# A folded DFT with its even rows split twice more, and one of its three products made once for seven sequences

## The chip, the cores and the metric

One core of a Trainium2 chip. The metric is the device time of one execution in microseconds (us). Before the change it is 2174.62 us, the median of three runs (2173.83 to 2174.92). The engines are named as in the profile: PE (matrix multiply), PEld (the weight loads of PE), DVE (vector), ACT (scalar), POOL (GpSimd), SP (the queue that issues most transfers).

## What is computed

Eight sequences of 3008 rows by 256 columns get a Fourier transform over the rows and one over the columns, of which the real part is kept. The result goes through two matrices with a squared ReLU in between.

```python
X = np.fft.fft(x, axis=1)            # x: (8, 3008, 256)
X = np.fft.fft(X, axis=2)
h = X.real.reshape(24064, 256) @ w_in        # (256, 2048)
g = np.maximum(h, 0.0) ** 2
out = g @ w_out                              # (2048, 256)
```

## The kernel before, in words

The transform over the 256 columns is folded into `w_in` at the start: `G1` and `G2` (128 and 127 rows by 2048) and a column `gE`. What is left of the transform is the DFT over the row index n, made separately for each sequence b.

**Symmetry.** The host lays the rows out so that row n comes with its three mirror rows (S - n, S/2 - n, S/2 + n), 1024 numbers in all, for n = 0 to 752. `fold` (six pieces `f_s` to `f_q` for each row tile, all on DVE) adds and subtracts these mirrors and the two column halves. It leaves two operands for each row tile: `wP` with 128 columns and one more (column H), and `wQ` with 127; each has an index `kp` for even and odd output frequency k.

**Products.** `dft_ops(b)` makes six groups: for kp = 0 and 1, three products named by `which`: 0 gives P (from `wP` and the cosine table), 1 gives Q (`wQ`, sine table), 2 gives E. E is one column, column H of `wP`, broadcast to 128 columns of weights so that its result stands on all 128 partitions. The rows lie as all even n (377) and then all odd n (376), three tiles of up to 128 rows each. In a group, `even_n` multiplies the three even tiles into a PSUM tile `pd` of 377 or 376 columns and ACT copies it to `da`; `odd_n` multiplies the three odd tiles, and DVE writes the sum of the two halves (L267) and, mirrored, their difference (L270, L272) into `Pt`, `Qt` or `Et`, tiles of 1505 columns in pairs of buffers (pool `pq`).

**Main loop.** There are 384 steps: 8 sequences by 6 blocks of 250 or 251 frequencies by 8 values of j. A step has `front` (two halves; each half multiplies G1 by Pt and G2 by Qt into PSUM tile `ph`, L292 and L293, and DVE forms `he` = Et * gE + P, then the two `g`, L295 to L298), `combine` (ACT: ReLU and square; POOL: four sums), and, two steps later, `back` (seven products with `w_out`, L332). After the last j of a block, `gather` combines the accumulators, and `store` transposes on PE (`po`, L366), copies on ACT (`os`, L368), and sends four transfers on SP (L370).

**What sets the order.** Each engine runs its instructions in the order of the program. The fold and the products of sequence b + 1 are a list of side pieces, each with a weight (0.7 for `f_s`, 1.2 for `odd_n`, and so on). `between`, called after each half of `front`, pops pieces at an even pace, so that the list is empty six halves before the sequence ends. Steps 0 to 7 of sequence 0 have no side pieces: there DVE prepares `w_out` (`load_wout`). The side work of sequence 0 itself (`ahead(0)`) runs before the main loop, with nothing beside it.

`pd` and `po` share two PSUM buffers (pool `psd`); `ph` has two of its own. Tiles of x stand in four buffers (`NX = 4`): `f_d` of tile t issues the load of tile t + 4 on SP (for sequence 0: on POOL's queue). SP issues in order too, and a transfer there waits until the one eight places ahead of it has landed.

Of the kernel before, what the change touches and what calls it, by code (L numbers as in the profile page):

```python
# [26 lines left out]

def row_tiles(S):  # L30

    q = S // 4
    tiles, at = [], 0
    for count in (q // 2 + 1, q // 2):
        assert 2 * P < count <= 3 * P
        for r in range(0, count, P):
            tiles.append((at + r, min(P, count - r)))
        at += count
    return tiles


@with_exitstack
def kernel(
# [23 lines left out]
    NT = 6  # L67
    NX = 4
    NK = (S // 8 + 1, S // 8)
    TILES = row_tiles(S)  # L70
    assert D == 2 * P and S % 16 == 0 and len(TILES) == NT and NROW == S // 4 + 1

    ctx.enter_context(tc.manual_schedule())
    const = ctx.enter_context(tc.tile_pool(name="const", bufs=1))
# [8 lines left out]
    op = ctx.enter_context(tc.tile_pool(name="op", bufs=2))  # L83
    psh = ctx.enter_context(tc.tile_pool(name="psh", bufs=2, space=PSUM))
# [7 lines left out]
    xt = {}  # L92

    def load_x(b, t):
        r0, rows = TILES[t]
        xt[b, t] = xp.tile([P, 4, D], F32, name="xt", tag="x")
        (nc.sync if b else nc.gpsimd).dma_start(out=xt[b, t][0:rows], in_=x[b, r0:r0 + rows])
# [4 lines left out]
    cosT = const.tile([P, 2, NT, NK[0]], F32, name="cosT")  # L102
    sinT = const.tile([P, 2, NT, NK[0]], F32, name="sinT")
# [11 lines left out]
    for kp in range(2):  # L115
        for tab, src in ((cosT, cos_s), (sinT, sin_s)):
            nc.gpsimd.dma_start(out=tab[:, kp], in_=src[:, kp])

    make_identity(nc, ident)

# [66 lines left out]

    folded = {}
    PQE = {}

    def fold(b, t):


        rows = TILES[t][1]
        r = slice(0, rows)
        st = {}

        def new(pool, nm, shape):
            st[nm] = pool.tile(shape, F32, name=nm, tag=nm)
            return st[nm]  # L200

        def f_s():
            v = xt[b, t]
            tt(out=new(fp, "fs", [P, 2, D])[r], in0=v[r, 0::2], in1=v[r, 1::2], op=ALU.add)

        def f_d():
            v = xt[b, t]
            tt(out=new(fp, "fd", [P, 2, D])[r], in0=v[r, 0::2], in1=v[r, 1::2], op=ALU.subtract)
            if b * NT + t + NX < B * NT:
                load_x(*divmod(b * NT + t + NX, NT))  # L210

        def f_sc():
            s, sc = st["fs"], new(fp, "sc", [P, 2, H + 1])
            nc.vector.tensor_copy(sc[r, :, 0:H + 1:H], s[r, :, 0:H + 1:H])
            tt(out=sc[r, :, 1:H], in0=s[r, :, 1:H], in1=s[r, :, D - 1:H:-1], op=ALU.add)

        def f_dc():
            d = st["fd"]
            tt(out=new(fp, "dc", [P, 2, H - 1])[r], in0=d[r, :, 1:H], in1=d[r, :, D - 1:H:-1], op=ALU.subtract)

        def f_p():
            sc, wP = st["sc"], new(wp, "wP", [P, 2, H + 1])
            for kp in range(2):
                tt(out=wP[r, kp], in0=sc[r, 0], in1=sc[r, 1], op=ALU.subtract if kp else ALU.add)

        def f_q():
            dc, wQ = st["dc"], new(wp, "wQ", [P, 2, H - 1])
            for kp in range(2):
                tt(out=wQ[r, kp], in0=dc[r, 0], in1=dc[r, 1], op=ALU.add if kp else ALU.subtract)
            folded[b, t] = (st["wP"], wQ)  # L230

        return [(0.7, f_s), (0.7, f_d), (0.5, f_sc), (0.4, f_dc), (0.6, f_p), (0.6, f_q)]

    def dft_ops(b):

        ops = []
# [5 lines left out]
        def group(kp, which, st):  # L242
            nk = NK[kp]
            n = P - 1 if which == 1 else P
            tab = sinT if which == 1 else cosT

            def product(half):
                ps = psd.tile([P, 512], F32, name="pd", tag="d")[0:n, 0:nk]
                for i in range(3):
                    t = 3 * half + i  # L250
                    rows = TILES[t][1]
                    w = folded[b, t][which % 2][0:rows, kp]
                    w = w[:, H:H + 1].to_broadcast([rows, n]) if which == 2 else w[:, 0:n]
                    nc.tensor.matmul(ps, w, tab[0:rows, kp, t, 0:nk],  # L254
                                     start=i == 0, stop=i == 2)
                return ps

            def even_n():
                ps = product(0)
                st["a"] = hp.tile([P, NK[0]], F32, name="da", tag="da", bufs=2)[0:n, 0:nk]  # L260
                nc.scalar.copy(st["a"], ps)

            def odd_n():
                ps = product(1)
                a, dst = st["a"], PQE[b][which]
                nh = S // 8
                tt(out=dst[:, kp:kp + 2 * nk - 1:2], in0=a, in1=ps, op=ALU.add)  # L267
                hi = dst[:, M - kp - 2 * (nh - 1):M - kp + 1:2][:, ::-1]
                if which == 1:
                    tt(out=hi, in0=ps[:, 0:nh], in1=a[:, 0:nh], op=ALU.subtract)  # L270
                else:
                    tt(out=hi, in0=a[:, 0:nh], in1=ps[:, 0:nh], op=ALU.subtract)  # L272
# [6 lines left out]
        return [(0.0, start)] + ops  # L279


    def front(b, k0, n, j, between):
# [194 lines left out]
```

## Time and profile before

| | before |
|---|---|
| median of three runs | 2174.62 us |
| the profiled execution | 2173.86 us, span 2172.1 us |
| PE busy | 2072.0 us, 95% of the span, 9504 matmuls |
| PEld busy | 1771.0 us, 82% |
| DVE busy | 1318.1 us, 61% |
| POOL busy | 1192.6 us, 55% |
| ACT busy | 927.5 us, 43% |

The sum of an engine's busy time over the span hides the stages: until about 115 us the kernel prepares `w_in`, folds sequence 0 and makes its products; until about 188 us it runs the first eight steps while DVE prepares `w_out`; from there on it is the main loop. Each product in fp32 shows in the profile as two matmul instructions and two weight loads, so 9504 matmuls are 4752 products. Matmuls overlap in the profile (a mean of 375 ns stands beside 212 ns from one start to the next), so PE's time is read from starts.

### The profile page before, as it was taken

The page shows a single profiled execution, that of the slowest core. Times are in us where ns is not written, and L with a number is a line of the kernel's source. Part 1 is how long each engine was busy: PE and PEld are TensorE (multiplying, and loading weights), DVE is VectorE, ACT ScalarE, POOL GpSimd, SP SyncE. Part 2 cuts the span into 40 slices and gives each one's busy share as a digit, 9 for nine tenths or more (in the row PEclk, how much of TensorE's full clock was granted, in tenths as well). Part 3 has the DMA queues.
Part 4 walks back from the last instruction along what each step waited for, and adds up shares of the span by engine and source line. Part 5 has one row for each costly group of instructions (what it writes and reads, how often), then busy time and mean ns, then how long its engine had stood idle before and what let it go on. Part 6 is the DMA issues. An engine that isn't in the chain of part 4 may idle for free.

```text
span 2172.1 us, 26892 instructions
## 1 busy us (share of the span) xinstructions
PE 2072.0 (95%) x9504; PEld 1771.0 (82%) x9504; DVE 1318.1 (61%) x3124; ACT 927.5 (43%) x1017; POOL 1192.6 (55%) x1776
## 2 busy tenths in 40 slices
PE   3668999999999999999999999999999999999998
PEld 1347888888888887888888888888888888888887
DVE  5588764677447764577546774477645775455553
ACT  0013443444445443444434444354434444344543
POOL 0046664566446654566545664466545665456655
PEclk8689999999999999999999999999999999999999
DMA  5211000111000100011001110011000000000000
GB/s 206 76 39 48 30 29 10 33 35 39 10 10 29 46 22 10 20 38 29 20 10 31 37 38 10 10 29 45 23 10 20 29 11 10 10 20 10 20 10 19
DMA packets 38371, 64.31 MB, mean 30 GB/s; under 512 B 3285, under 2 KB 27605, under 8 KB 37725
## 3 DMA queue, kind: packets, MB, share of 16 engines
q1 hardware_dynamic: 35981, 54.63, 8.3%
q0 software_dynamic: 1440, 7.72, 1.0%
q8 instruction: 74, 1.21, 0.2%
q14 instruction: 60, 0.49, 0.1%
q10 hardware_dynamic: 816, 0.26, 0.1%
HBM read 37.96 MB, written 24.64 MB: 29 GB/s over the span
## 4 chain that ended last, share of the span: by engine, by line
PE 93%; DVE 6%; issue 0%; ACT 0%; DMA 0%; POOL 0%; POOLq 0%; DVEq 0%
PE mC L332 15%; PE mA L332 15%; PE mB L332 15%; PE ph L293 15%; PE ph L292 15%; PE pd L254 8%; PE mD L332 7%; PE po L366 2%; PE pg L167 1%; DVE fs L153 1%; DVE fs L145 1%; DVE fs L139 1%; DVE fd L144 1%; DVE fs L151 0%; DVE fd L149 0%; DVE fd L143 0%
## 5 line engine op out<-in xcount | busy, mean ns | idle before, releaser
L295 DVE SCALAR_TENSOR_TENSOR he<-Et,gE,ph 128x251 f32<-128x251 f32 (+1 forms) x768 | 362.8, 472 | 673.9 <-PE ph L293 673.0
L306 ACT ACTIVATE g<-g 128x1004 f32<-128x1004 f32 (+1 forms) x384 | 399.4, 1040 | 825.1 <-DVE g L298 656.7
L312 POOL TENSOR_TENSOR s<-g 128x251 f32<-128x251 f32 (+1 forms) x384 | 243.4, 634 | 750.7 <-ACT g L307 671.0
L292 PE MATMUL ph<-Pt,G 128*128 128x251 f32 (+1 forms) x1536 | 455.6, 378 | 28.0 <-DVE g L298 27.9
L293 PE MATMUL ph<-Qt,G 127*128 127x251 f32 (+1 forms) x1536 | 455.4, 377 | 0.0
L307 ACT ACTIVATE g<-g 128x1004 f32<-128x1004 f32 (+1 forms) x384 | 399.2, 1040 | 12.2
L332 PE MATMUL mC<-s,wsum 128*128 128x251 f32 (+1 forms) x1536 | 390.3, 375 | 0.0
L332 PE MATMUL mA<-g,wout 128*128 128x251 f32 (+1 forms) x1536 | 389.9, 375 | 0.0
L297 DVE TENSOR_TENSOR g<-he,ph 128x251 f32<-128x251 f32 (+1 forms) x768 | 320.5, 417 | 58.8 <-DVE he L295 0.5
L292 PEld LDWEIGHTS ph<-Pt,G 128*128 128x128 f32 x1536 | 290.7, 190 | 77.8 <-DVE g L298 33.3
L293 PEld LDWEIGHTS ph<-Qt,G 127*128 127x128 f32 x1536 | 293.8, 191 | 36.9
L332 PEld LDWEIGHTS mA<-g,wout 128*128 128x128 f32 x1536 | 288.0, 190 | 42.2
L332 PEld LDWEIGHTS mC<-s,wsum 128*128 128x128 f32 x1536 | 291.9, 190 | 35.7
L298 DVE TENSOR_TENSOR g<-he,ph 128x251 f32<-128x251 f32 (+1 forms) x768 | 314.1, 409 | 0.0
L313 POOL TENSOR_TENSOR s<-s,g 128x251 f32<-128x251 f32 (+1 forms) x384 | 284.7, 741 | 30.1
L314 POOL TENSOR_TENSOR s<-g 128x251 f32<-128x251 f32 (+1 forms) x384 | 289.2, 753 | 0.0
L315 POOL TENSOR_TENSOR s<-g,s 128x251 f32<-128x251 f32 (+1 forms) x384 | 259.8, 676 | 0.0
L332 PE MATMUL mB<-g,wsum 128*128 128x251 f32 (+1 forms) x768 | 225.4, 374 | 0.0
L332 PE MATMUL mD<-s,wout 128*128 128x251 f32 (+1 forms) x768 | 225.0, 374 | 0.0
L332 PE MATMUL mB<-s,wout 128*128 128x251 f32 (+1 forms) x768 | 224.6, 374 | 0.0
L332 PEld LDWEIGHTS mB<-g,wsum 128*128 128x128 f32 x768 | 146.1, 190 | 17.9
L332 PEld LDWEIGHTS mD<-s,wout 128*128 128x128 f32 x768 | 144.9, 189 | 18.1
(63 smaller groups left out, 1351.5 us busy)
## 6 DMA issues: line engine op xcount, KB each, us to landing
xt<-in_x_dram SPq DMA_DIRECT2D x28, 512.0 KB
out_dram<-os SPq DMA_DIRECT2D x96, 125.0 KB
out_dram<-os SPq DMA_DIRECT2D x80, 126.0 KB
raw<-in_moe_w_in_dram SPq DMA_DIRECT2D x8, 512.0 KB
raw<-in_moe_w_out_dram SPq DMA_DIRECT2D x8, 512.0 KB
xt<-in_x_dram SPq DMA_DIRECT2D x7, 484.0 KB
xt<-in_x_dram SPq DMA_DIRECT2D x7, 480.0 KB
cosT<-in_cos_s_dram POOLq DMA_DIRECT2D x2, 1131.0 KB, 17.7
```

The lines of the kernel that those rows point to most:

```text
L292: nc.tensor.matmul(hP, G1[:, fs], pt[:, ks], start=True, stop=True)
L293: nc.tensor.matmul(hQ, G2[:, fs], qt[:, ks], start=True, stop=True)
L295: nc.vector.scalar_tensor_tensor(out=t, in0=et[:, ks], scalar=gE[:, fc:fc + 1], in1=hP, op0=ALU.mult, op1=ALU.add)
L297: tt(out=g[:, h, 0, 0:n], in0=t, in1=hQ, op=ALU.add)
L298: tt(out=g[:, h, 1, 0:n][:, ::-1], in0=t, in1=hQ, op=ALU.subtract)
L306: act(v, v, AF.Relu)
L307: act(v, v, AF.Square)
L312: gt(out=s1, in0=g21, in1=g22, op=ALU.add)
L313: gt(out=s2, in0=s1, in1=g11, op=ALU.subtract)
L314: gt(out=s3, in0=g11, in1=g21, op=ALU.subtract)
L315: gt(out=s4, in0=g12, in1=s2, op=ALU.subtract)
L332: nc.tensor.matmul(acc[nm][:, i, 0:n], w, v[:, 0:n], start=j == 0 and i == 0, stop=j == NJ - 1, skip_group_check=True)
```

## The change

**Rows in four classes.** `class_tiles` sorts the rows by n: n mod 8 = 0 (95 rows, one tile), n mod 8 = 4 (94 rows, one tile), n mod 4 = 2 (188 rows: tiles of 128 and 60), n odd (376 rows: 128, 128, 120). The layout in DRAM stays; the loads of x take every fourth or second row of the even part. So there are seven tiles of each sequence, not six, and `fold` runs once more for each sequence.

**Products in four pieces.** `even_n` makes three products into one PSUM tile `pd`: class 0 and class 1 with 95 (94) columns each, class 2 with 189 (188); ACT copies the first of them only. `join_4` (DVE) makes sum and mirrored difference of class 0 and 1 (to `db`), `join_2` those of `db` and class 2 (to `dc2`), and `odd_n` those of `dc2` and the odd rows, as before. `pd` is held from `even_n` to `join_2`.

**E in one pass.** For sequence 0, E is made as before. For sequences 1 to 7, `load_column` fetches column H of all seven sequences, number by number (28 transfers on SP, four in each of steps 8 to 14 of the program), `fold_column` folds it, and `dft_ops(None)` makes two groups with weights of seven columns. The result `e_rows` (7 x 1505) goes to DRAM (`e_dram`), and `load_e(b)` reads one row of it back to 128 partitions as `Et`. So a sequence has four groups, not six; sequence 1's list of side pieces has those two groups more, seven `fold_column` pieces and the write of `e_dram`.

**Buffers and tables.** x has three buffers (`NX = 3`). The tables are loaded class by class on POOL's queue in 24 transfers, not 4.

```diff
-    NX = 4
+    NX = 3
+    TILES = class_tiles(S)
+    NT = len(TILES)
...
-        r0, rows = TILES[t]
+        _, r0, step, rows = TILES[t]
         xt[b, t] = xp.tile([P, 4, D], F32, name="xt", tag="x")
-        (nc.sync if b else nc.gpsimd).dma_start(out=xt[b, t][0:rows], in_=x[b, r0:r0 + rows])
+        (nc.sync if b else nc.gpsimd).dma_start(out=xt[b, t][0:rows], in_=x[b, r0:r0 + step * (rows - 1) + 1:step])
...
+    def load_column(t):
+        _, r0, step, rows = TILES[t]
+        xe[t] = const.tile([P, 4, NE], F32, name=f"xe{t}")
+        for i in range(4):
+            nc.sync.dma_start(out=xe[t][0:rows, i], in_=x[1:B, r0:r0 + step * (rows - 1) + 1:step, i, H].rearrange("b r -> r b"))
+
+    def fold_column(t):
+        r = slice(0, TILES[t][3])
+        v = xe[t]
+        s = hp.tile([P, 2, NE], F32, name="es", tag="es", bufs=2)
+        tt(out=s[r], in0=v[r, 0::2], in1=v[r, 1::2], op=ALU.add)
+        we[t] = const.tile([P, 2, NE], F32, name=f"we{t}")
+        for kp in range(2):
+            tt(out=we[t][r, kp], in0=s[r, 0], in1=s[r, 1], op=ALU.subtract if kp else ALU.add)
...
             def even_n():
-                ps = product(0)
-                st["a"] = hp.tile([P, NK[0]], F32, name="da", tag="da", bufs=2)[0:n, 0:nk]
-                nc.scalar.copy(st["a"], ps)
+                st["ps"] = psd.tile([P, 512], F32, name="pd", tag="d")[0:n]
+                a = st["a"] = hp.tile([P, 2 * P], F32, name="da", tag="da", bufs=2)[0:n]
+                for c, at, nk in ((0, 0, n2), (1, n2, n2), (2, 2 * n2, n1)):
+                    product(st["ps"][:, at:at + nk], c)
+                nc.scalar.copy(a[:, 0:n2], st["ps"][:, 0:n2])
...
+            def join_4():
+                a, ps = st["a"], st["ps"]
+                st["b"] = hp.tile([P, 2 * P], F32, name="db", tag="db", bufs=2)[0:n, 0:n1]
+                both(st["b"][:, 0:n2], st["b"][:, n2:n1], a[:, 0:n2], ps[:, n2:2 * n2])
+
+            def join_2():
+                a, ps = st["b"], st["ps"]
+                st["c"] = hp.tile([P, NC[0][3]], F32, name="dc2", tag="dc2", bufs=2)[0:n, 0:n0]
+                both(st["c"][:, 0:n1], st["c"][:, n1:n0], a, ps[:, 2 * n2:2 * n2 + n1])
...
-            return [(0.6, even_n), (1.2, odd_n)]
+            return [(0.5, even_n), (0.5, join_4), (0.7, join_2), (1.2, odd_n)]
...
-            for which in range(3):
-                ops += group(kp, which, {})
+            for which in ((2,) if b is None else (0, 1) if b else (0, 1, 2)):
+                ops += group(kp, which)
+        if b is None:
+            ops.append((0.0, lambda: nc.sync.dma_start(out=e_dram[:, :], in_=e_rows)))
+        return ops
+
+    def load_e(b):
+        nc.sync.dma_start(out=PQE[b][2], in_=e_dram[b - 1:b].to_broadcast([P, NKT]))
...
     def ahead(b):
-        return [piece for t in range(NT) for piece in fold(b, t)] + dft_ops(b)
+        ops = [piece for t in range(NT) for piece in fold(b, t)] + dft_ops(b)
+        if b == 1:
+            ops += [(0.6, lambda t=t: fold_column(t)) for t in range(NT)] + dft_ops(None)
+        return ops + [(0.0, lambda: load_e(b))] if b else ops
...
+            if NJ <= i < NJ + NT:
+                load_column(i - NJ)
```

Three places show how instructions move. The first is PE at the end of the preparation, where the groups of sequence 0 are made (`pd`) and the main loop begins (`ph`). Before:

```order
L172 MATMUL pe<-altd,win 128x1 x8
L254 MATMUL pd<-cosT,wP 128x377 x6
L254 MATMUL pd<-sinT,wQ 127x377 x6
L254 MATMUL pd<-cosT,wP 128x377 x6
L254 MATMUL pd<-cosT,wP 128x376 x6
```

and now:

```order
L215 MATMUL pe<-altd,win 128x1 x8
L317 MATMUL pd<-cosT,wP 128x95 x2
L317 MATMUL pd<-cosT,wP 128x189 x2
L317 MATMUL pd<-cosT,wP 128x377 x3
L317 MATMUL pd<-sinT,wQ 127x95 x2
L317 MATMUL pd<-sinT,wQ 127x189 x2
L317 MATMUL pd<-sinT,wQ 127x377 x3
```

A group of six products of 377 columns has become seven: two of 95 columns, two of 189 and three of 377. All groups of all sequences have this form; those of E for sequences 1 to 7 have 7 output rows instead of 128.

The second is SP from the last loads of `w_out` (`raw`) to the first stores (`out_dram`), that is steps 8 to 14, where the tiles of sequence 1 are fetched (`xt`). Before:

```order
L128 DMA raw<-in_moe_w_out_dram 128x2x512 x8
L97 DMA xt<-in_x_dram 128x1024
L370 DMA out_dram<-os 126x256
L370 DMA out_dram<-os 125x256
L370 DMA out_dram<-os 126x256
L370 DMA out_dram<-os 124x256
L97 DMA xt<-in_x_dram 120x1024
```

and now (`xe` are the column's numbers, rows by sequences):

```order
L171 DMA raw<-in_moe_w_out_dram 128x2x512 x8
L243 DMA xe_954<-in_x_dram 95x7x1 x4
L133 DMA xt<-in_x_dram 60x1024
L243 DMA xe_994<-in_x_dram 94x7x1 x4
L243 DMA xe_1049<-in_x_dram 128x7x1 x4
L243 DMA xe_1092<-in_x_dram 60x7x1 x4
L133 DMA xt<-in_x_dram 128x1024
L455 DMA out_dram<-os 126x256
L455 DMA out_dram<-os 125x256
L455 DMA out_dram<-os 126x256
L455 DMA out_dram<-os 124x256
L243 DMA xe_1151<-in_x_dram 128x7x1 x4
```

The load of sequence 1's fifth tile (128 rows) and the stores of the first block now stand behind 16 transfers of single numbers; 12 more stand behind those stores.

The third is SP at the end of sequence 0, from the last stores of its fifth block on. Before:

```order
L370 DMA out_dram<-os 126x256
L370 DMA out_dram<-os 125x256
L97 DMA xt<-in_x_dram 128x1024
L370 DMA out_dram<-os 125x256 x2
L370 DMA out_dram<-os 124x256
L370 DMA out_dram<-os 125x256
```

and now:

```order
L455 DMA out_dram<-os 126x256
L455 DMA out_dram<-os 125x256
L360 DMA e_dram<-e_rows 7x1505
L364 DMA Et<-e_dram 128x1505
L133 DMA xt<-in_x_dram 60x1024
L455 DMA out_dram<-os 125x256 x2
```

The write of `e_dram` and the read of `Et` stand between the two stores; by the pace of the side pieces both are issued in step 45 of the 48, and `Et` is first read by DVE in the first step of sequence 1. For the later sequences the read alone stands there, issued in step 44.

More of the change, by code (lines that the diff above doesn't have):

```diff
@@ L39, in row_tiles, with class_tiles, column_counts, table_places @@
     return tiles
+def class_tiles(S):
+    half = S // 8 + 1
+    tiles = []
+    for c, order in enumerate((range(0, half, 4), range(2, half, 4), range(1, half, 2), range(half, S // 4 + 1))):
+        for r in range(0, len(order), P):
+            tiles.append((c, order[r], order.step, len(order[r:r + P])))
+    return tiles
+def column_counts(S):
+    counts = []
+    for kp in range(2):
+        n0 = len(range(kp, S // 4 + 1, 2))
+        n1 = (n0 + 1) // 2
+        n2 = (n1 + 1) // 2
+        counts.append((n2, n2, n1, n0))
+    return counts
+def table_places(S):
+    places, at = [], 0
+    for c, *_ in class_tiles(S):
+        places.append(at)
+        at += column_counts(S)[0][c]
+    return places, at
 @with_exitstack
@@ L83 @@
     op = ctx.enter_context(tc.tile_pool(name="op", bufs=2))
+    dp = ctx.enter_context(tc.tile_pool(name="dp", bufs=1, space=bass.MemoryType.DRAM))
     psh = ctx.enter_context(tc.tile_pool(name="psh", bufs=2, space=PSUM))
@@ L101 @@
     altd = const.tile([P, 2, 1], F32, name="altd")
-    cosT = const.tile([P, 2, NT, NK[0]], F32, name="cosT")
-    sinT = const.tile([P, 2, NT, NK[0]], F32, name="sinT")
+    cosT = const.tile([P, 2, WT], F32, name="cosT")
+    sinT = const.tile([P, 2, WT], F32, name="sinT")
     wout = const.tile([P, 2, NJ, D], F32, name="wout")
@@ L114 @@
         load_x(0, t)
-    for kp in range(2):
+    for t, (c, r0, step, rows) in enumerate(TILES):
         for tab, src in ((cosT, cos_s), (sinT, sin_s)):
-            nc.gpsimd.dma_start(out=tab[:, kp], in_=src[:, kp])
+            for i, (s0, count) in enumerate(row_tiles(S)):
+                mine = [r for r in range(count) if (s0 + r - r0) % step == 0 and 0 <= (s0 + r - r0) // step < rows]
+                if mine:
+                    o = (s0 + mine[0] - r0) // step
+                    nk = NC[0][c]
+                    nc.gpsimd.dma_start(out=tab[o:o + len(mine), :, PLACE[t]:PLACE[t] + nk],
+                                        in_=src[mine[0]:mine[-1] + 1:step, :, i, 0:nk])
     make_identity(nc, ident)
@@ L234, in dft_ops @@
     def dft_ops(b):
-        ops = []
         def start():
@@ L263, in odd_n @@
             def odd_n():
-                ps = product(1)
-                a, dst = st["a"], PQE[b][which]
+                ps = psd.tile([P, 512], F32, name="pd", tag="d")[0:n, 0:n0]
+                product(ps, 3)
+                dst = e_rows if b is None else PQE[b][which]
                 nh = S // 8
[L267 to L272, printed above, removed]
```

51 lines of the change are left out of this document (31 added, 20 removed).

## The prediction

> **What bounds the kernel now.** I read the page's part 1 first, then busy time by stretches of the span, then the list of waits, and only then single instructions in order of time. Part 1, and then four rows by stretches (from and to, length, then busy time with counts for PE, PEld, DVE, ACT, POOL, the granted clock, DMA share, GB/s):
>
> ```profile
> PE 2072.0 (95%) x9504; PEld 1771.0 (82%) x9504; DVE 1318.1 (61%) x3124; ACT 927.5 (43%) x1017; POOL 1192.6 (55%) x1776
> ```
>
> ```profile
> 77.40:95.00 17.60, 8.03 (x11) 2.80 (x12) 17.26 (x55) 0.47 (x1) 1.09 (x2) 0.60 0.50 156
> 95.00:116.00 21.00, 21.00 (x63) 12.40 (x62) 5.03 (x10) 2.36 (x5) 0.00 (x0) 0.93 0.19 66
> 195.00:275.00 80.00, 80.00 (x386) 71.21 (x385) 61.45 (x146) 39.70 (x43) 53.94 (x77) 1.00 0.13 40
> 1100.00:1400.00 300.00, 299.32 (x1382) 256.26 (x1381) 175.92 (x424) 134.70 (x149) 168.26 (x250) 1.00 0.08 23
> ```
>
> From about 195 us on PE is never idle and has its full clock, and DVE is busy 77% where sequence 1's side pieces run at their densest, 59% later. All PE waits of the loop are these two rows (total us, times, longest), and most of the first lies in the eight steps before 195 us:
>
> ```profile
> PE ph L292 <- DVE g L298: 27.9, 8, 5.7
> PE po L366 <- ACT os L368: 4.7, 7, 0.7
> ```
>
> So in the loop a microsecond of PE work taken away is a microsecond of span, until something else becomes late. Before the loop it is DVE's fold (77 to 95 us) and then PE's products (95 to 116 us) that set the pace.
>
> **What a product costs.** Matmul durations overlap, so I take starts. Six pd instructions, which are three products of 377 columns, and what follows; eight instructions of the transposes, which are four products of 128 columns; and, from the preparation, products of one column each with its own weight load:
>
> ```profile
> 38.45 1.84 PE L172 MATMUL pe<-altd,win 128*128 128x1 f32 x16
> ...
> 1041.09 1.04 PE L366 MATMUL po<-ident,c 128*126 128x128 f32 x8
> 1041.96 1.01 PE L332 MATMUL mA<-g,wout 128*128 128x251 f32 x4
> 1042.81 0.59 PE L332 MATMUL mB<-g,wsum 128*128 128x251 f32 x2
> ...
> 1051.31 2.07 PE L254 MATMUL pd<-cosT,wP 128*128 128x377 f32 x6
> 1053.22 1.01 PE L332 MATMUL mA<-g,wout 128*128 128x251 f32 x4
> ```
>
> 377 columns: 1.91 / 3 = 0.637 us. 251 columns: 0.85 / 2 = 0.425. Both are 1.69 ns a column. 128 columns: 0.87 / 4 = 0.218. One column: 1.84 / 8 = 0.23, so below some 128 columns the 128 columns of weights set the time, at 0.22. For 189 columns I take 0.320 (by columns), for 95 columns 0.22: by columns it would be 0.161, which is the lower bound, and the 0.425 of the 251-column product is an upper one for both. 0.22 has the nearest rows on both sides.
>
> **PE work in the loop.** The rows of the pd line give 576 instructions, so 288 products, 36 for each sequence:
>
> ```profile
> L254 PE MATMUL pd<-cosT,wP x384: 477/479/997, 79.9 to 1900.6; 128*128 128x377 f32 x64, 128*128 128x376 f32 x64, 121*128 121x377 f32 x16, 120*128 120x377 f32 x16
> L254 PE MATMUL pd<-sinT,wQ x192: 477/479/835, 95.7 to 1883.6; 128*127 128x377 f32 x64, 128*127 128x376 f32 x64, 121*127 121x377 f32 x16, 120*127 120x377 f32 x16
> ```
>
> A group costs 6 x 0.637 = 3.82 us before, and 2 x 0.22 + 2 x 0.320 + 3 x 0.637 = 2.99 now. The loop holds the groups of sequences 1 to 7: 42 before (160.5 us), 28 + 2 = 30 now (89.7 us; the two with seven weight columns stream as many columns). That is **-71 us**. With the lower bound for 95 columns it is -78, with the upper bound for both small products (group 3.61) -52.
>
> Had E stayed, 42 groups of 2.99 would have taken 35 us off; E's twelve groups fewer are the other half.
>
> **Before the loop: -1 us.** A tile's fold takes 2.9 us here, from one `fs` to the next, and there is a seventh:
>
> ```profile
> 77.45 0.69 DVE L204 TENSOR_TENSOR fs<-xt 128x512 f32<-128x512 f32 x1
> ...
> 80.35 0.68 DVE L204 TENSOR_TENSOR fs<-xt 128x512 f32<-128x512 f32 x1
> ...
> 94.31 1.63 PE L254 MATMUL pd<-cosT,wP 120*128 120x377 f32 x2 [1.26 <-DVE wP L224]
> ...
> 115.84 0.59 PE L292 MATMUL ph<-Pt,G 128*128 128x251 f32 x2
> ```
>
> The last product of the first group then starts 2.9 us later, at 97.2, and the five groups behind it take 5 x 0.83 = 4.2 us less: -1.3. Here the joins stand bare. A full-width join is 0.55 us on DVE, and the smallest operation of the fold 0.17:
>
> ```profile
> 78.67 0.17 DVE L214 COPY sc<-fs 128x4 f32<-128x4 f32 x1
> ...
> 96.05 0.55 DVE L267 TENSOR_TENSOR Pt<-da,pd 128x377 f32<-128x377 f32 x1 [1.18 <-PE pd L254]
> ```
>
> The four narrower joins lie between these two, so DVE needs 1.8 to 3.3 us for a group that takes PE 2.99. At the upper end PE waits for a PSUM buffer, 0.3 us in each of six groups, and some for the chain's latencies: bounds -3 and +4, taken -1. The 24 table loads on POOL's queue cost it 20 issues more at 0.53 us, 11 us, long before their first use at 79 us.
>
> ```profile
> 3.52 0.53 POOL L117 DMA_DIRECT2D cosT<-in_cos_s_dram  x1
> ...
> 79.05 0.55 POOL L97 DMA_DIRECT2D xt<-in_x_dram  x1 [72.83 <-DVE sc L214]
> ```
>
> ```profile
> xt<-in_x_dram POOLq DMA_DIRECT2D x1, 484.0 KB, 11.0
> xt<-in_x_dram POOLq DMA_DIRECT2D x1, 480.0 KB, 4.5
> ```
>
> With three x buffers the fourth tile is asked for at 79.05, lands 4.5 us later (alone on the queues; 11.0 was at the start, with everything in flight), and is wanted at 77.45 + 3 x 2.9 = 86.1. In the loop a load has more than 30 us. No cost.
>
> **DVE in sequence 0's loop: +2 us.** The loop's own work on DVE is these three in each half step (mean ns of one):
>
> ```profile
> L295 DVE SCALAR_TENSOR_TENSOR he<-Et,gE,ph 128x251 f32<-128x251 f32 (+1 forms) x768 | 362.8, 472 | 673.9 <-PE ph L293 673.0
> L297 DVE TENSOR_TENSOR g<-he,ph 128x251 f32<-128x251 f32 (+1 forms) x768 | 320.5, 417 | 58.8 <-DVE he L295 0.5
> L298 DVE TENSOR_TENSOR g<-he,ph 128x251 f32<-128x251 f32 (+1 forms) x768 | 314.1, 409 | 0.0
> ```
>
> The side list of sequence 1 weighs 46.1, where it weighed 31.8, over the same 40 steps: 1.45 times as dense. A step is 11 products of 0.425, so 4.68 us. In the 80 us from 195 the loop's own DVE work is 17.1 steps with two halves of 472 + 417 + 409 ns, 44 us, and 3 us of `gather`; 14 us are side pieces. At 1.45 times, DVE is busy 67 of 80 us, 84%. PE keeps two ph buffers ahead, so a burst is felt only where two pieces fall into one half. Bounds 0 and +10 (two waits of the 5.7 us above); taken +2. In the other six loops the side list weighs 36.1 over 48 steps, less dense than that of sequence 1 before (0.40 against 0.43 for each half), at which PE did not wait.
>
> **E through DRAM: +1 us.** Write and read are issued in step 45; until the first step of sequence 1 there are 2.5 to 3 steps, 12 to 14 us. `Et` is 753 KB: by the 480 KB row 7.1 us, by the 484 KB row 17 us; the write of 42 KB at most 4.5. Cover is just there; without it DVE's `he` waits, behind it every `g`, and PE after two ph products: at most some 8 us, once. Sequences 2 to 7 need only the read, with 15 us of cover. Likewise small: `pd` held while a `store` comes leaves one buffer for its two `po`; that happens in one place (step 27 of sequence 0), for one wait of the 0.7 us kind.
>
> **Column loads: 0.** 752 rows x 28 = 21,056 transfers of 4 bytes. The nearest row is the ACT queue in the first 5 us, where half-KB pieces and single numbers flow (packets, MB, share of 16 engines):
>
> ```profile
> q10 hardware_dynamic: 294, 0.14, 10.3%
> ```
>
> and the page's own rows for the whole span, where q1 is SP's queue:
>
> ```profile
> q1 hardware_dynamic: 35981, 54.63, 8.3%
> out_dram<-os SPq DMA_DIRECT2D x96, 125.0 KB
> out_dram<-os SPq DMA_DIRECT2D x80, 126.0 KB
> out_dram<-os SPq DMA_DIRECT2D x16, 124.0 KB
> xt<-in_x_dram SPq DMA_DIRECT2D x28, 512.0 KB
> xt<-in_x_dram SPq DMA_DIRECT2D x7, 484.0 KB
> xt<-in_x_dram SPq DMA_DIRECT2D x7, 480.0 KB
> raw<-in_moe_w_in_dram SPq DMA_DIRECT2D x8, 512.0 KB
> raw<-in_moe_w_out_dram SPq DMA_DIRECT2D x8, 512.0 KB
> ```
>
> 0.103 x 16 x 5 us / 294 = 28 ns a packet, the upper end; the lower is 0, and I take half, 14 ns, since 4 bytes are less than 512. Over all 16 engines the columns are 18 to 37 us, spread over seven steps (33 us). But they aren't spread evenly. Of q1's 35,981 packets, 24,064 are rows of out, 5271 rows of x and 4096 pieces of weights. 2550 are left over, and that is exactly what comes out if a transfer runs on as many engines as the largest divisor of its rows up to 16, with one closing packet on each: 125 rows on 5 (96 of these), 126 on 14, 124 on 4, 121 on 11, 120 on 15, 128 on 16. So the 95-row column goes over five engines and the 94-row one over two: 4 x (133 + 329 + 56 + 28 + 56 + 56 + 56) = 2856 numbers pass the busiest engine. The load of sequence 1's fifth tile stands behind 2184 of them. At 14 ns that is 31 us after step 8; the tile is wanted in step 19, 51 us after it. At 28 ns it is 61 us, and the sixth tile and the stores (two `os` buffers, ACT waiting in order) are late too: +16 us, the upper bound.
>
> The Trainium skill, "DMA: Bandwidth & Descriptors", section "Why a DMA increments its semaphore by 16 and not by 1", states this same divisor rule, and the 2550 packets agree with it. Its section "Rules for kernel authors" speaks against this change: a non-contiguous last dimension becomes one descriptor for each element and should be rearranged. No row here shows so many at once.
>
> **Sum.** -71 - 1 + 2 + 1 = -69, on the profiled execution's 2173.86: 2104.9. The median of the runs stands 0.76 above it: 2105.6, say **2106 us**, 3.2% faster.
>
> **Rivals.**
>
> *PE stays busy, but the joins leak (12%).* PSUM buffers are held over two to five halves, and each group's next product waits for `join_2`, DVE's joins for ACT's copy behind two activations. For it: three waits between engines where there was one. Against it: the copy's inputs come two halves earlier than its reader. Price: 30 groups x 0.7 us, the longest wait of this kind above, is 21 us: 2127.
>
> *Columns a little late (7%).* The 28 ns of the row: +16 us, 2122.
>
> *Columns dear (7%), slower than before.* For it: the two engines, and that transfers queue in order, so that x and the stores stand behind the columns. Against it: 28 ns is already a mean over larger packets. The columns end after 2856 numbers at a cost c each, 66 us (14 steps) may pass before the sixth tile is wanted, and the gain of 69 is gone where 2856 c - 66 = 69 us: from 47 ns on. At 60 ns the stall is 105 us: 2210.
>
> *Small products by columns (4%).* The 95-column products cost 0.161, PE saves 78 us, and the preparation -3: 2095. Against it: the 0.23 us of the one-column products.
>
> The forecast has the remaining 70%, from 2098 (the preparation at -3, DVE at 0, the 95-column products nearly half-way to 0.161) to 2114 (DVE at its upper bound).
>
> **Range and chances.** From 2098 to 2130: it holds the forecast, the leak, the mildly late columns and the upper bound of the small products (-52: 2125), and leaves out the dear columns and most of the last case. A difference of 0.2% (4 us) is what a measurement can tell. Faster 0.92, slower 0.07, and 0.01 between, where the columns cost just about 47 ns.
>
> **What the changed profile would show.** Right: three products of class 0 to 2 that start 0.22, 0.22, 0.32 us apart; 252 pd products in place of 288; PE busy at 99% or more in every stretch of the loop, DVE at 84% near 200 to 275 us; `ph` first at about 115 us. Wrong: DVE rows `fs` waiting for DMA `xt`, or ACT `os` waiting for its stores, between 240 and 330 us (the columns); DVE `he` waiting for DMA `Et` at a sequence's start (E); PE `pd` or `po` waiting for DVE joins or ACT in the loop (the leak). A loop in which PE is idle more than 2% would make the forecast wrong.

## The result: 2125.0 us, 2.3% faster, 19 us above the forecast

| | before | after |
|---|---|---|
| median | 2174.77 us (4 runs) | 2125.0 us (4 runs, 2123.76 to 2126.03) |
| ratio | | 0.9772, 95% interval 0.9755 to 0.9789 |
| span of the profiled execution | 2172.1 us | 2124.2 us |
| first `ph` | 115.84 us | 119.58 us |
| sequence 0 from step 8 to the first `ph` of sequence 1 | 215.7 us | 216.7 us |
| one of the sequences 1 to 6, from first `ph` to first `ph` | 253.5 us | 244.8 us |

The last three rows are differences of starts in the trace. They say where the 47.9 us of span went: 52.1 us were gained in the sequences 1 to 6 (8.7 in each) and 0.4 in the last one; 3.7 us were lost before the loop and 1.0 in sequence 0. Medians here and below are of the fast runs: one run of e_alone (3482 us) and one of efirst (4289 us) were far slower and do not count in them.

The profile of after, part 1, which answers to the first row of the prediction:

```profile
PE 2012.9 (95%) x9432; PEld 1740.2 (82%) x9432; DVE 1371.1 (65%) x3337; ACT 916.4 (43%) x1005; POOL 1223.2 (58%) x1797
```

72 matmul instructions fewer are 36 products fewer, 252 of `pd` where there were 288, as the prediction said. The table by stretches (from and to, length, then PE, PEld, DVE, ACT, POOL, granted clock, DMA share, GB/s), the stretches set at the same events as before: the fold, the products behind it, the dense side pieces, the middle of the loop:

```profile
78.40:98.20 19.80, 6.43 (x13) 2.85 (x13) 19.56 (x62) 0.24 (x1) 2.25 (x4) 0.59 0.37 117
98.20:119.60 21.40, 21.40 (x73) 13.05 (x74) 11.62 (x37) 1.19 (x5) 0.00 (x0) 0.82 0.30 85
195.00:275.00 80.00, 79.91 (x383) 70.55 (x383) 68.58 (x161) 37.83 (x41) 54.77 (x76) 1.00 0.28 47
1100.00:1400.00 300.00, 297.98 (x1420) 261.28 (x1419) 192.55 (x474) 137.89 (x151) 180.88 (x265) 1.00 0.09 29
```

DVE rose to 68.58 of 80 us, 86% (forecast 84%), and PE stayed busy beside it. In the middle of the loop PE was idle for 2.0 us of 300, where it had been 0.7. The second row shows the stage before the loop: its 21.4 us are what the same stage took before (94.3 to 115.8), at a lower mean clock (0.82, before 0.92).

The waits of PE (total us, times, longest):

```profile
PE ph L377 <- DVE g L383: 29.1, 8, 5.7
...
PE po L451 <- ACT os L453: 10.1, 15, 0.7
```

The first row is the one of before (27.9, 8, 5.7). The second was 4.7 us in 7 waits. No wait of PE for the new joins stands in the list inside the loop.

Two costs in the trace are larger than the forecast had them. The first is a group's first half. Here are the products of `even_n` for one group of sequence 2 in order of time (start, duration, engine, operation; x8 instructions are four products of 95, 94, 128 and 60 rows):

```profile
616.09 1.44 PE L317 MATMUL pd<-sinT,wQ 95*127 95x94 f32 x8
617.46 0.69 PE L377 MATMUL ph<-Pt,G 128*128 128x250 f32 x2
617.99 0.38 PE L378 MATMUL ph<-Qt,G 127*128 127x250 f32 x1
```

From the first start to that of `ph` it is 1.37 us, where 2 x 0.22 + 2 x 0.320 = 1.08 was forecast. The records of weight loads by shape (busy us, mean ns, then idle time before them and what ended it):

```profile
L317 PEld LDWEIGHTS pd<-sinT,wQ 60*127 60x127 f32 x32 | 4.9, 192 | 3.7 <-issue 3.7
```

The 60-row loads are as long as others, but the engine that loads stands idle before them, 3.7 us in 32, though nothing in the profile holds it. The single starts show what that costs. By columns, two instructions of 188 or 189 columns would start 0.16 us apart, as they do in cut65 below. Here the distance is 0.25 us from a 128-row one to a 60-row one, 0.26 between two 60-row ones, and 0.25 from a 60-row one to whatever follows: 0.28 us more. The product that follows is late once more: its two instructions start 0.32 us apart, and 0.21 elsewhere. Together that is 0.385 us for each group, so that a group costs 3.37 us.

The second is the store, where `pd` leaves one PSUM buffer for both `po`. PE in order of time, then ACT and DVE at the same place:

```profile
627.75 2.06 PE L317 MATMUL pd<-sinT,wQ 128*127 128x376 f32 x6
629.65 0.60 PE L451 MATMUL po<-ident,c 128*126 128x128 f32 x4
630.93 0.66 PE L451 MATMUL po<-ident,c 128*126 128x128 f32 x4 [0.68 <-ACT os L453]
631.42 1.01 PE L417 MATMUL mA<-g,wout 128*128 128x250 f32 x4
```

```profile
630.29 0.58 ACT L453 COPY os<-po 126x512 f32<-126x512 f32 x1 [2.85 <-PE po L451]
```

```profile
629.85 0.55 DVE L330 TENSOR_TENSOR Qt<-dc,pd 127x376 f32<-127x376 f32 x1 [0.28 <-PE pd L317]
630.32 0.54 DVE L332 TENSOR_TENSOR Qt<-pd,dc 127x376 f32<-127x376 f32 x1
```

`odd_n` was issued just ahead of `store`. Its `pd` holds one of the two `psd` buffers until DVE's second join ends at 630.86; the first `po` has the other until ACT's copy ends at 630.87. The second `po` starts at 630.93 and not at 629.65 + 2 x 0.22 = 630.09: 0.84 us lost.

Six of the fifteen waits are of this kind, with `odd_n` just ahead of the store, and so were all seven of before. In the other nine the `pd` of an `even_n` is still held for its joins, as the prediction said of step 27 of sequence 0. It happens in steps 27, 35 and 43 of sequence 0, and in step 35 of each of the sequences 1 to 6. At 338 us, PE, ACT and DVE:

```profile
338.00 0.66 PE L451 MATMUL po<-ident,c 128*126 128x128 f32 x4 [0.68 <-ACT os L453]
```

```profile
337.36 0.58 ACT L453 COPY os<-po 126x512 f32<-126x512 f32 x1 [2.74 <-PE po L451]
```

```profile
338.02 0.35 DVE L332 TENSOR_TENSOR dc<-pd,db 127x188 f32<-127x188 f32 x1
```

PE goes on 0.06 us behind ACT's copy, while DVE's `join_2` is still reading `pd`. Both kinds cost 0.84 us: fifteen are 12.6 us in the whole kernel; the seven of before were 5.9.

### The profile page after: what moved, and what is told of

The parts are those of the page before. It is cut to its first block, busy times and chain, and to the rows that moved or that the text cites. A ratio compares the mean times of both kernels' runs of the same rounds, so it can differ in the third digit from the quotient of the medians.

```text
span 2124.2 us, 26994 instructions
## 1 busy us (share of the span) xinstructions
PE 2012.9 (95%) x9432; PEld 1740.2 (82%) x9432; DVE 1371.1 (65%) x3337; ACT 916.4 (43%) x1005; POOL 1223.2 (58%) x1797
## 4 chain that ended last, share of the span: by engine, by line
PE 92%; DVE 7%; ACT 0%; issue 0%; DMA 0%; POOL 0%; POOLq 0%; ACTq 0%; DVEq 0%
PE ph L377 15%; PE mA L417 15%; PE mC L417 15%; PE mB L417 15%; PE ph L378 15%; PE mD L417 7%; PE pd L317 6%; PE po L451 2%; PE pg L210 1%; DVE fs L196 1%; DVE fs L188 1%; DVE fd L187 1%; DVE fs L182 1%; DVE fs L194 0%; ACT os L453 0%; DVE fd L192 0%
## 5 line engine op out<-in xcount | busy, mean ns | idle before, releaser
L397 POOL TENSOR_TENSOR s<-g 128x251 f32<-128x251 f32 (+1 forms) x384 | 252.0, 656 | 687.2 <-ACT g L392 653.1
L378 PE MATMUL ph<-Qt,G 127*128 127x251 f32 (+1 forms) x1536 | 455.6, 377 | 0.0
L378 PEld LDWEIGHTS ph<-Qt,G 127*128 127x128 f32 x1536 | 294.5, 192 | 36.6
L399 POOL TENSOR_TENSOR s<-g 128x251 f32<-128x251 f32 (+1 forms) x384 | 290.5, 757 | 0.0
```

The costliest lines, as they stand in the source:

```text
L378: nc.tensor.matmul(hQ, G2[:, fs], qt[:, ks], start=True, stop=True)
L397: gt(out=s1, in0=g21, in1=g22, op=ALU.add)
L399: gt(out=s3, in0=g11, in1=g21, op=ALU.subtract)
```

## The experiments

Each was timed in several rounds beside the kernel before on the same chip; its median was 2174.77 us beside after, 2174.79 beside the next four and 2174.83 beside the others. Medians with the ratio to it:

| kernel | median us | ratio, 95% interval | span us |
|---|---|---|---|
| after | 2125.0 | 0.9772 [0.9755, 0.9789] | 2124.2 |
| cut65 | 2115.7 | 0.9727 [0.9713, 0.9742] | 2113.8 |
| cut64 | 2125.0 | 0.9771 [0.9757, 0.9786] | 2122.9 |
| hold21 | 2111.4 | 0.9710 [0.9695, 0.9724] | 2109.9 |
| e_alone | 2125.2 | 0.9772 [0.9753, 0.9792] | 2122.8 |
| cut65_hold21 | 2100.1 | 0.9658 [0.9644, 0.9673] | 2097.9 |
| split_alone | 2169.6 | 0.9975 [0.9966, 0.9985] | 2166.1 |
| before_hold | 2167.7 | 0.9968 [0.9956, 0.9981] | 2165.3 |
| efirst | 2089.4 | 0.9606 [0.9590, 0.9622] | 2087.9 |

### Is it the rows of the small tile? cut65 and cut64

The 188 rows of class 2 are cut differently; the number of products, their columns and the data stay the same.

```diff
-        for r in range(0, len(order), P):
-            tiles.append((c, order[r], order.step, len(order[r:r + P])))
+        step = 123 if c == 2 else P
+        for r in range(0, len(order), step):
+            tiles.append((c, order[r], order.step, len(order[r:r + step])))
```

That is cut65: 123 and 65 rows in place of 128 and 60. In cut64 the number is 124, so 124 and 64 rows.

> The change with its 188 rows of class 2 cut into tiles of 123 and 65 rows, not 128 and 60; nothing else. Theory (rows): a tile of at most 64 rows makes PE load its weights without overlap. In the changed kernel's loop the 189-column instructions of such a group take 253, 264 and 250 ns to the next start where 189 columns at 0.845 ns are 160, together 0.29 us a group. Expected: all of these at 160 to 190 ns, 28 groups x 0.29 = 8 us less in the loop, 1.5 less before it: 2115 (2113 to 2117). Rival (short products): products of 189 columns cost 0.25 us for each instruction whatever their rows; then no difference from 2125.

> The same cut one row away: tiles of 124 and 64 rows. Theory (rows, with the limit at 64): as slow as the change, 2125 (2123 to 2127), with 250 to 264 ns again. Rival (few rows cost, without a limit): close to the kernel with 65 rows, within 2 us of it.

cut65 took 2115.7 us, 9.3 less than after; cut64 2125.0, no difference. A single row decides. The same group of sequence 2 in cut65, and its weight loads:

```profile
613.39 1.25 PE L318 MATMUL pd<-sinT,wQ 95*127 95x94 f32 x8
614.48 0.59 PE L378 MATMUL ph<-Pt,G 128*128 128x250 f32 x2
614.90 0.59 PE L379 MATMUL ph<-Qt,G 127*128 127x250 f32 x2
```

```profile
L318 PEld LDWEIGHTS pd<-sinT,wQ 65*127 65x127 f32 x32 | 5.9, 199 | 0.0
```

In cut64:

```profile
614.57 1.44 PE L318 MATMUL pd<-sinT,wQ 95*127 95x94 f32 x8
615.94 0.69 PE L378 MATMUL ph<-Pt,G 128*128 128x250 f32 x2
616.47 0.59 PE L379 MATMUL ph<-Qt,G 127*128 127x250 f32 x2
```

```profile
615.43 0.29 PEld L318 LDWEIGHTS pd<-sinT,wQ 64*127 64x127 f32 x2 [0.22 <-issue]
```

With 65 rows the four products take 1.09 us, the 1.08 of the forecast, and the loads follow each other without a gap (0.0 idle in 32). With 64 rows it is 1.37 us again, as with 60. So the forecast's prices for 95 and for 189 columns were right, and the cost lies in the number of rows. From the group's first start to that of the second product behind it (L379 here, L378 in after) it is 1.51 us, where after has 1.90: 0.39 us. The loop agrees: each of the sequences 1 to 6 has four such groups and takes 243.24 us, 1.54 less than in after, which is 4 x 0.385. Sequence 0 is 1.3 us shorter from step 8 on, so that the loop gained 10.6 us; the spans differ by 10.4, the medians by 9.3.

### Is it the store? hold21

`between` holds a piece back when a store is near: `even_n` two steps ahead or less, `odd_n` one step ahead or less.

```diff
+        due = (3 - i) % NJ
         while side and spent <= 0:
+            name = side[0][1].__name__
+            if name == "even_n" and due <= 2 or name == "odd_n" and due <= 1:
+                return
             t, f = side.pop(0)
```

> The change, but a group's even_n is not begun in the two steps before a store or in its step, and odd_n not in the step before or in its step, so that both transposes of a store find their own free PSUM buffer. Theory (leak at the stores): 15 waits of PE for the copy of os, 0.75 us each, go: PE po <- ACT os from 10.1 us on PE (and the weight loads' 13.7) to 0, the time 10 to 11 us lower, 2114 to 2115. Rival (the pieces held back only come bunched elsewhere and DVE makes PE wait there): within 3 us of 2125, with PE ph <- DVE g above 35 us.

2111.4 us, 13.6 less than after. That is more than the 10 to 11 expected, which went by 0.75 us a wait; by the starts, 15 x 0.84 are 12.6. PE's waits, cut to those for DVE's `g` and those of `po`, and then the store of the same block in order of time:

```profile
PE ph L377 <- DVE g L383: 29.1, 8, 5.7
...
PE po L451 <- POOL c L438: 2.5, 1, 2.5
```

```profile
621.79 1.04 PE L451 MATMUL po<-ident,c 128*126 128x128 f32 x8
```

No wait for ACT's copy is left (the wait for POOL is the last store of the kernel and stands in before too), and the eight instructions of the store run in one piece.

### The two halves of the change: e_alone and split_alone

e_alone is the kernel before with E in one pass: its six tiles and two classes, groups of 6 x 0.637 us, three x buffers, but columns, `fold_column`, `e_dram` and `load_e` of the change. Its result stands in the first rows of sequence 1's `Et`, not in a tile of its own, before it goes to DRAM. split_alone is the change without the pass: E is made for each sequence, with no columns and no transfers through DRAM.

```diff
 # e_alone, beside the new functions of the change
+    return [(0 if r0 <= S // 8 else 3, r0, 1, rows) for r0, rows in row_tiles(S)]
 # split_alone
-            for which in ((2,) if b is None else (0, 1) if b else (0, 1, 2)):
+            for which in range(3):
...
-            if NJ <= i < NJ + NT:
-                load_column(i - NJ)
```

> The kernel before, with E of seven sequences in one pass and through DRAM, but rows in two classes as before (six tiles, groups of six products of 377 columns) and three x buffers. Theory: twelve groups fewer of 3.82 us, 45.8 us, and nothing given back except up to 2 us in sequence 0's loop: 2129 to 2131. Rival (the columns or the trip through DRAM cost in the loop of sequence 0 or at its end): above 2135.

> The change without its E pass: rows in four classes, three groups of seven products for each kp of every sequence as E is made for each sequence. Theory: a group costs 3.28 us as measured in the change, not 3.82, 42 groups in the loop, 23 us less; against it 14 more waits at the stores of 0.84 us, 12 us, 3.7 us before the loop, and some 1 us in the loop of sequence 0: 2168 (2164 to 2172), so that nearly all of the change's gain is the E pass. Rival (the split carries half of the gain, as the forecast had it): 2140 or less.

E alone takes 2125.2 us, as much as the whole change and 4 us less than was expected of it; the split alone takes 2169.6, 5 us less than before. PE's waits at stores in e_alone, and in split_alone:

```profile
PE po L427 <- ACT os L429: 0.7, 1, 0.7
```

```profile
PE po L451 <- ACT os L453: 13.5, 20, 0.7
```

So E's pass gives more than its arithmetic: twelve groups of 3.82 us are 45.8, and six waits fewer than before (7 to 1) are 5.0, 50.8 in all for a measured 49.6. Which pieces fall beside a store changes with the list, and here it changed for the better. The split is the reverse. Its 42 groups save 35 us by the forecast; the small tile takes 42 x 0.385 = 16.2 back, thirteen waits more take 10.9, and its first `ph` comes at 118.27, 2.4 us late. That leaves 5.5 us, and 5.2 are measured.

### Both mends: cut65_hold21

> Both mends on the change: class 2 as tiles of 123 and 65 rows, and the pieces held back around a store. Theory (two separate costs on PE): they add up, 9.3 and 13.6 us as measured one by one, 2102 (2100 to 2104). Rival (the two overlap, or DVE or the start of the loop becomes the limit): 2106 or more.

2100.1 us, 24.9 below after, where 9.3 and 13.6 are 22.9. In the loop they add exactly: the sequences 1 to 6 are 3.33 us shorter than in after, and apart it was 1.54 and 1.79. But for the last store, the only waits of PE in its loop are the ones in the steps before 195 us:

```profile
PE ph L378 <- DVE g L384: 28.8, 8, 5.8
```

Each of the sequences 1 to 6 takes 241.45 us in it, 12.0 less than before. Two groups fewer (2 x 3.82) and four cheaper by 0.83 account for 11.0 of them, and the one wait of before for 0.84; 0.2 us are left over.

### Did the kernel before have the same leak? before_hold

The lines of hold21, put into the kernel before.

> The kernel before with nothing but even_n and odd_n held back around a store in the same way. Theory: its 7 waits at the stores cost 0.84 us each, 6 us less: 2169 (2167 to 2171). Rival (holding back itself speeds up or slows down something else): outside of that.

2167.7 us, 7.1 less than before (seven waits by 0.84 are 5.9). The wait of 4.7 us that the prediction quoted was a cost of before, not the background of the loop:

```profile
PE ph L292 <- DVE g L298: 27.8, 8, 5.7
...
PE po L366 <- POOL c L353: 2.5, 1, 2.5
```

### A version beyond both: efirst

The E pass is moved out of sequence 0's loop into the preparation: it is made for all eight sequences; the columns are loaded between pieces of `w_in`, folded in DVE's stretch of its third chunk, and multiplied where PE waits for DVE. Class 2 is cut 96 + 92, and the stores are held as above.

```diff
-    NE = B - 1
+    NE = B
...
+        for t in {1: (0, 1), 2: range(2, NT)}.get(c, ()):
+            load_column(t)
+        if c == 3:
+            for _, f in e_ops[:4]:
+                f()
...
+        if c == 2:
+            for t in range(NT):
+                fold_column(t)
...
-    for _, f in ahead(0):
+    first = ahead(0)
+    for _, f in first[:6] + e_ops[4:] + first[6:]:
```

> Class 2 as tiles of 96 and 92 rows, pieces held back as before, and E made for all eight sequences in one pass during the preparation: the column's numbers are loaded between the pieces of w_in, folded while DVE waits for PE there, and the two groups run while PE waits for DVE. Theory: against 2102 for both mends, the two E groups leave the loop (5.9 us) and two groups of sequence 0 leave the preparation (6.8 us), with up to 2.5 us of DVE joins added there: 2092 (2088 to 2096). Rival (the column loads delay w_in, on which DVE waits in the preparation): above 2098.

2089.4 us, 10.7 below cut65_hold21 and 3.9% below before. The stretch of the preparation that took up the work, in efirst and then in after:

```profile
40.00:80.00 40.00, 21.58 (x92) 12.23 (x91) 26.96 (x73) 3.38 (x7) 0.57 (x1) 0.74 0.40 51
```

```profile
40.00:80.00 40.00, 16.97 (x59) 9.75 (x59) 21.70 (x43) 2.50 (x5) 0.00 (x0) 0.66 0.05 14
```

PE and DVE were idle for 23 and 18 of these 40 us in after; in efirst they do 4.6 and 5.3 us more in the same time. The first `ph` comes at 113.72 us (117.53 in cut65_hold21), and sequence 0 from step 8 takes 205.1 us (212.0): the two E groups, at the 3.27 us each that they take in cut65, are 6.5 of these 6.9. The other sequences take the same 241.45 us in both.

## Why the prediction was right, and where it was not

**The form of the argument held.** A microsecond of PE work taken from the loop was a microsecond of span, and nothing else became the bound. 2125.0 is inside the range; it is 19 us above the forecast, and in the spans the loss is 21.1 us: -47.9 measured, -69 by the sum. (The profiled execution of after was 1.0 us above its median, that of before 0.9 below.)

**"What a product costs", the 0.320 for 189 columns: this step failed.** For 95 columns 0.22 held, for 377 columns 0.637 too (627.75 to 629.65 is 1.90 for three). The 189-column products were priced by columns alone; with 60 rows one of the two costs 0.385 us more, between itself and its neighbours. A group was 3.37 us and not 2.99. In "PE work in the loop" the -71 was therefore mis-sized: 30 x 0.385 = 11.5 us of it were not there. cut65 shows it. The prediction's upper bound for both small products, by which -71 becomes -52, contained this, but it was set by the 251-column row, and not by any thought of rows. That the loop's measured gain is 52.1 + 0.4 is chance: part of it is the next point.

**"That happens in one place", one more wait of `po`: this step failed.** The prediction looked at the list of sequence 0 and costed the wait by the page's 0.7 us. The place that it named is there, but a `pd` held for its joins meets a store in nine places, and one meeting of the kind that before had is gone: eight waits more than before, at 0.84 us each, are 6.7 us against the 0.7 in the +1. That `pd` is held through three pieces was seen; that two more stores of sequence 0 and one in each of the sequences 1 to 6 meet it was not. The rival "the joins leak" named the right pool and the wrong reader. It had each group's own next product wait for `join_2`, and no such wait shows inside the loop; `po` waits instead, for ACT's copy, which the prediction had named as a sign of the leak. Its time of 2127 is near the result by chance: the waits are 12.6 us in all, not 21 more, and the small tile is no part of it.

**"Before the loop: -1": wrong in sign.** The first `ph` came 3.7 us later. The rows of after: fold, last product of the first group, the last two groups and first `ph`:

```profile
78.45 0.69 DVE L266 TENSOR_TENSOR fs<-xt 95x512 f32<-95x512 f32 x1
```

```profile
98.15 1.63 PE L317 MATMUL pd<-cosT,wP 120*128 120x377 f32 x2 [1.26 <-DVE wP L286]
...
112.84 3.53 PE L317 MATMUL pd<-sinT,wQ 95*127 95x94 f32 x14
116.21 3.54 PE L317 MATMUL pd<-cosT,wP 95*128 95x94 f32 x14
119.58 0.59 PE L377 MATMUL ph<-Pt,G 128*128 128x251 f32 x2
```

The fold began 1.0 us later (78.45, before 77.45). That is not the change's doing: in cut65 it began at 78.95, in cut65_hold21 at 77.40. The seventh tile cost its 2.9 us (19.70 from fold to last product, 16.86 before). But the five groups behind it took 21.43 us, and before 21.53: the 4.2 us of the forecast did not come. The clock tells half of it. In after and then in before, two stretches around its rise:

```profile
104.00:106.00 2.00, 2.00 (x5) 1.08 (x4) 0.00 (x0) 0.00 (x0) 0.00 (x0) 0.56 0.18 58
106.00:108.00 2.00, 2.00 (x11) 1.35 (x10) 1.12 (x3) 0.24 (x1) 0.00 (x0) 1.00 0.13 50
```

```profile
96.00:98.00 2.00, 2.00 (x4) 1.08 (x4) 1.01 (x2) 0.00 (x0) 0.00 (x0) 0.52 0.99 357
98.00:100.00 2.00, 2.00 (x8) 1.14 (x7) 0.00 (x0) 0.47 (x1) 0.00 (x0) 1.00 0.47 180
```

PE has a granted clock of 0.50 until about 105.8 us in after, until about 97.9 in before. Behind the first group that is 7.6 us at half speed, where it was 3.6: 2.0 us more lost. At full clock a group takes 3.37 us here (from 112.84 to 116.21), 0.38 over the 2.99 of the forecast; for five that is an estimated 1.9, and the two make 3.9 of the 4.1 us that are missing. Only part of it is the small tile's: from fold to first `ph` it is 40.9 to 41.1 us in the four kernels that split the rows and have a tile of 60 or 64 (after, cut64, hold21, split_alone), and 40.1 and 40.4 in the two with 65. Why the clock rose later was not tested. It goes with the rows in four classes: in these six it rose between 104.2 and 106.3 us, in before, before_hold and e_alone between 97.9 and 98.4. The forecast priced five groups at the loop's pace, in a stage whose quoted row had a clock of 0.93.

**"DVE in sequence 0's loop: +2": right.** By the sum, sequence 0 was to be 2 us shorter from step 8 on (six groups cheaper by 0.83, less 2 and 1). It was 1.0 longer, but with both mends, that is without the small tile and the waits at stores, it takes 212.0 us, 3.7 less than before, where one wait at a store was in it. So DVE at 86% and E together cost at most 5.0 + 0.8 - 3.7 = 2.1 us of the 3 that were forecast.

**"E through DRAM", the transfer itself: right, no cost.** SP's queue in order of time:

```profile
391.47 0.27 SPq L360 DMA_DIRECT2D e_dram<-e_rows  x1
393.50 0.35 SPq L364 DMA_DIRECT2D Et<-e_dram  x1
```

DVE's list of waits has no row that names DMA `Et`.

**"Column loads: 0": right.** From 190 to 250 us, DMA activity in 40 slices of 1.5 us, then packets, then SP's queue:

```profile
DMA  0000023111116759983577857200000181000000
...
DMA packets 19786, 2.45 MB, mean 41 GB/s; under 512 B 18843, under 2 KB 19344, under 8 KB 19780
...
q1 hardware_dynamic: 19780, 2.37, 30.3%
```

The columns pass between 197 and 229 us, and no row of DVE's waits names DMA `xt` or `xe`. 0.303 x 16 x 60 us / 19,780 = 14.7 ns a packet, rows of x included; taken were 14, and the gain would have been gone from 47 on. By the rule of the Trainium skill's "DMA: Bandwidth & Descriptors", section "Rules for kernel authors", such an access should have been rearranged. The trace agrees that it makes single numbers of it, 18,843 packets under 512 bytes, but here they cost the span nothing.

**"E's twelve groups fewer are the other half": wrong as a statement of where the gain is.** By the sum, split and E were 35 us each. Alone, E gives 49.6 and the split 5.2; and on top of E the split gives 0.2. It takes its own gain back through the small tile, the waits at stores and the later start. With both mends the split is worth 25 us on top of E, its full 30 x 0.83 = 24.9.

**Where the 19 us are.** In the spans: 11.5 us for groups of 3.37 us in the loop, 6.7 - 0.7 = 6.0 for the waits at stores, 3.7 + 1 = 4.7 before the loop (1.0 of it the later fold). The last sequence is 0.4 us shorter, which makes 21.8, for 21.1 measured; the 0.7 too many may lie in sequence 0, where DVE and E together came out below their forecast. What they did cost there is in part a third thing. PE's last pause before the dense stretch is longer than before, and PE comes back from it at half its clock. After, by stretches of 2 us, then before, then cut64:

```profile
188.00:190.00 2.00, 0.00 (x0) 0.00 (x0) 1.97 (x3) 0.00 (x0) 1.73 (x2) 1.00 0.00 0
...
192.00:194.00 2.00, 2.00 (x6) 1.59 (x6) 1.02 (x3) 1.15 (x2) 0.41 (x1) 0.50 0.00 0
```

```profile
186.00:188.00 2.00, 0.08 (x1) 0.09 (x1) 1.87 (x5) 0.00 (x0) 1.22 (x4) 1.00 0.00 0
...
192.00:194.00 2.00, 2.00 (x11) 1.78 (x10) 1.30 (x2) 1.66 (x2) 1.97 (x3) 1.00 0.00 0
```

```profile
192.00:194.00 2.00, 1.96 (x10) 1.65 (x10) 1.82 (x5) 1.75 (x2) 0.00 (x0) 1.00 0.05 12
```

Six instructions in 2 us, where there were eleven. cut65_hold21 has the same stretch at 190 to 192 us, so neither mend removes it. In cut64 the pause was 2.3 us, not 3.9, and the clock stayed at 1.00; its sequences 1 to 6 take the 244.8 us of after, but sequence 0 from step 8 takes 215.7 us, 0.9 less than in after. So the stretch at half clock is worth about 0.9 us, as far as one trace of each can tell.

**Two slips in the working.** With 0.161 us for the 95-column products "PE work in the loop" gives -74 (30 groups of 2.87 are 86.2), not -78. The rival "small products by columns" then stands near 2099, inside the range and not below it, and the 2098 of the forecast would need these products at 0.161 in full. And the 752 rows of the columns are 753. Neither bears on the steps that failed.

## What to carry to other kernels

Where a contraction would leave a tile of 64 rows or fewer between larger ones, try an evener cut: 123 + 65 in place of 128 + 60 took 9.3 us off here, for one changed number. Where products of side work share PSUM buffers with a store, look at what the list puts beside each store over the whole kernel, not at one place; holding a piece back by a step or two gave 13.6 us here, and 7.1 in the kernel before. And try the parts of a change alone: of two parts whose sums were equal, one had all of the gain, and the other was worth its sum only when what it leaked had been stopped.

## What the runs showed of the hardware that was not expected

A stationary tile of 64 rows or fewer made its neighbours dearer. With 65 rows four products in a row took 1.09 us, with 64 or 60 rows 1.37; starts were 0.25 to 0.26 us apart instead of 0.16 at three places, before, in and behind the pair, and the product behind it lost 0.10 us more between its two instructions. The weight load itself is no longer (192 ns against 199), it only begins late. The Trainium skill, "TensorE: Matmul & The Clock Gate", section "LDWEIGHTS (loading the stationary operand)", says that a load's time goes by its columns and not its rows. The records' durations agree; the starts show that the pace of a chain of products does not follow from it, and no run here shows why 64 is the limit. 64 and 65 rows are the only sizes tried right at it, for weights of 127 and 128 columns. In the two E groups of after the weights have seven columns: there the two 60-row instructions start 0.16 us apart, while the starts before and behind them stay at 0.25. These narrow weights showed two more things. Products of 95 columns started 0.17 us apart, by their columns, where they take 0.19 to 0.22 with weights of 127 or 128 columns. And the product behind a half group with narrow weights lost the same 0.10 us, in cut65 and e_alone too, where no tile has 64 rows or fewer.
